# Talking-heads attention with a PReLU layer behind it: another order inside an attention step, and v's products in both places of one step

## The chip, the cores and the metric

The kernel runs on one core of a Trainium2 chip. The metric is the time of one execution in microseconds (us) on the device; less is better. In the profile PE is the engine that multiplies matrices (PEld its loads of weights), DVE the vector engine, ACT the scalar engine, POOL GpSimd and SP the engine that only issues transfers here.

## What is computed

Four batches of 12 heads, 448 positions, 64 numbers a head. Scores of all heads are mixed over the heads before the softmax, the probabilities once more after it, and the result goes through two layers with a PReLU between them. The shapes and the calls around it are left out:

```python
def _attn_ref(q, k, v, w_pre, w_post):
    scale = 1.0 / np.sqrt(q.shape[-1])
    scores = scale * np.matmul(q, k.transpose(0, 1, 3, 2))
    scores = np.einsum('bhij,hg->bgij', scores, w_pre)
    scores = scores - np.max(scores, axis=-1, keepdims=True)
    attn = np.exp(scores)
    attn = attn / (np.sum(attn, axis=-1, keepdims=True) + 1e-09)
    attn = np.einsum('bhij,hg->bgij', attn, w_post)
    return np.matmul(attn, v).astype(np.float32)

def _moe_ref(x, w_in, w_out, alpha):
    h = x @ w_in
    g = np.maximum(h, 0.0) + alpha * np.minimum(h, 0.0)
    return (g @ w_out).astype(np.float32)
```

x is (1792, 768), w_in (768, 2048), w_out (2048, 768); w_in, w_out and alpha come as 64-bit floats.

## The kernel before

Two stages follow each other: attention, which leaves x in DRAM (`x2`), and the two layers, which read it. The change touches the first alone.

The rows of queries are cut into 16 chunks (4 a batch, of 120, 120, 120 and 97 queries), and a chunk into groups of 10 queries times 12 heads, 120 partitions. A step takes two groups, the pair m; there are 90 pairs, and a chunk has six (the last of a batch four and a half). What happens to a pair, and where it stands in the code:

- `qk` (L138) multiplies q and k of a chunk, two heads at a time, six calls a chunk, into the tile `s`, two PSUM banks, of which there is one buffer (`ps_s`). `qk_out` (L149) is ACT's copy of it into `st`; I call it the evict of the scores.
- `relay` (L158), issued by POOL, moves `st` into a layout where the heads lie on partitions: tile `sr`.
- `mix` (L165) mixes the heads on PE: tile `m`, two buffers. `rmax` (L174) takes the row's maximum on DVE, `exp` (L179) the exponential on ACT, one half of the pair a call, `norm` (L186) the sums and the scaled mixing weights `r` on DVE.
- `post` (L197) mixes the probabilities on PE, into the tile `pa`, of which there is one buffer; `post_out` (L208) copies it on ACT, two copies, into `at` of its chunk.
- `pv` (L217) multiplies `at` with v, once all pairs of a chunk are through, in two halves of 48 matmuls in the profile's count, into the same one buffer of `ps_s` that the scores use; `pv_out` (L232) copies the sums on ACT after the second half, and a transfer takes them to `x2`.

The order is written out by hand (`manual_schedule`): each engine works off its instructions in the order in which the code emits them. `step(m)` (L378) emits one step: mixing of pair m + 1, `post` of pair m - 2, `norm` of m - 1, `rmax` of m + 1, the two `exp` of pair m, and what stands in the step's two places, (m, 0) and (m, 1). A place holds a `qk` or a half of `pv`, or nothing; the table `places` (L285 to L298) says what. `use(place, 0)` emits the products on PE and `use(place, 1)` the copy on ACT. The scores of a later chunk and v's products of an earlier one are so woven into the steps of the present one. Between them DVE rounds the 64-bit weights (`convert`, L250) at a fixed number of instructions a step, and SP issues the loads.

Of the kernel before, what the change touches and what calls it, by code (L numbers as in the profile page):

```python
# [36 lines left out]
LAG = 2  # L37
# [24 lines left out]
def talking_heads_prelu(ctx: ExitStack, tc: tile.TileContext, q, k, v, w_pre, w_post, mask, w_in, w_out, alpha, out):  # L62
# [102 lines left out]
    def mix(m):  # L165

        ps = ps_m.tile([128, 2, 512], F32, tag="m", name=f"m{m}")
        ga, gb = sr_t.pop(2 * m), sr_t.pop(2 * m + 1)
        for hf, g in ((0, ga), (64, gb)):
            for u, r in ((0, slice(0, 64)), (1, slice(64, SR0 + GP))):  # L170
                nc.tensor.matmul(ps[hf:hf + 64, u, :S], wk[r, :], g[r, :], start=True, stop=True)  # L171
        m_t[m] = ps

    def rmax(m):  # L174
        nm = sm.tile([128, 2], F32, tag="nm", name=f"nm{m}")
        nc.vector.tensor_reduce(out=nm, in_=m_t[m][:, :, :S], axis=AX.X, op=ALU.max, negate=True)  # L176
        nm_t[m] = nm

    def exp(m, u):  # L179
        if u == 0:  # L180
            e_t[m] = ep.tile([128, 2, S], F32, tag="e", name=f"e{m}")
            se_t[m] = sm.tile([128, 2], F32, tag="se", name=f"se{m}")
        nc.scalar.activation(out=e_t[m][:, u], in_=m_t[m][:, u, :S], func=AF.Exp, bias=nm_t[m][:, u:u + 1], scale=1.0,  # L183
                             accum_out=se_t[m][:, u:u + 1])

    def norm(m):  # L186
        se = se_t.pop(m)
        s1 = sm.tile([128, 2], F32, tag="s1", name=f"s1{m}")
        nc.vector.tensor_scalar_add(s1, se, 1e-9)
        nc.vector.reciprocal(out=s1, in_=s1)  # L190
        r = rp.tile([128, 2, HP], F32, tag="r", name=f"r{m}")
        wf = wq.rearrange("p (o g) i -> p o (g i)", o=1)
        nc.vector.tensor_tensor(r, wf.to_broadcast([128, 2, HP]),
                                s1.rearrange("p (u o) -> p u o", o=1).to_broadcast([128, 2, HP]), ALU.mult)
        r_t[m] = r

    def post(m):  # L197
        e, r = e_t.pop(m), r_t.pop(m)
        for u in range(2):
            for jb in range(NJ):  # L200
                s, c = divmod(jb, 2)
                for g in range(2):
                    h = slice(64 * g, 64 * g + 64)
                    dst = pa[64 * c:64 * c + 64, g, s * GP:(s + 1) * GP].rearrange("p (h i) -> p h i", h=H)
                    nc.tensor.matmul(dst[:, :, HI * u:HI * u + HI], e[h, u, 64 * jb:64 * jb + 64],  # L205
                                     r[h, u].rearrange("p (h i) -> p h i", h=H), start=True, stop=True)

    def post_out(m):  # L208
        for g in range(2):
            n = 2 * m + g  # L210
            ci, r = groups[n]
            if n == first[ci]:
                a_t[ci] = ap_.tile([128, NS, H, CW], F32, tag="a", name=f"at{ci}")
            dst = a_t[ci].rearrange("p s h i -> p (s h) i")[:, :, r * GI:(r + 1) * GI]
            nc.scalar.copy(dst, pa[:, g, :NS * GP].rearrange("p (s i) -> p s i", i=GI))  # L215
# [69 lines left out]
    places = {}  # L285
    for ci in range(NC):
        m = (first[ci + 1] - 1) // 2 + LAG + 1
        places[m, 1], places[m + 1, 0] = ("pv", ci, 0), ("pv", ci, 1)
    for ci in range(1, NC):
        m1 = laid_out(first[ci]) - 1  # L290
        m0 = laid_out(first[ci - 1]) + 1 if ci > 1 else -1
# [17 lines left out]
    with tc.manual_schedule():  # L309
# [52 lines left out]
        def relays(upto, dmas):  # L362
            nonlocal relayed
            while relayed < min(upto, NG):
                relay(relayed, dmas[relayed % len(dmas)])
                relayed += 1
# [3 lines left out]
        live = lambda m: 0 <= m < NB  # L370

        def use(place, out):
            if place in places:
                f, *args = places[place]
                {"qk": (qk, qk_out), "pv": (pv, pv_out)}[f][out](*args)


        def step(m):  # L378


            nonlocal done
            for f, *args in jobs.get(m, []):
                f(*args)
            if live(m + 1):
                mix(m + 1)
            now, later[:] = list(later), []
            for f in now:
                f()
            if live(m - LAG):
                post(m - LAG)  # L390
            if live(m - 1):
                norm(m - 1)
            if live(m + 1):
                rmax(m + 1)
            if live(m):
                exp(m, 0)
            use((m - 1, 1), 1)
            if m >= 0:
                relays(2 * (m + 2 + RAHEAD) if m > 2 else first[1], (nc.gpsimd,))
            if live(m):  # L400
                exp(m, 1)
            use((m, 0), 0)
            if live(m - LAG):
                post_out(m - LAG)
            use((m, 0), 1)
            use((m, 1), 0)
            want = (m + 1) * conv_steps // (NB - 4)
            while done < want and done < conv_steps:
                next(conv, None)
                done += 1  # L410

        last = max(m for m, _ in places)
        for m in range(-1, max(NB + LAG, last + 1) + 1):
            step(m)
# [144 lines left out]
```

## Time and profile before

| what | value |
|---|---|
| median of 3 runs | 953.32 us (939.89 to 953.99) |
| the profiled execution | 943.48 us, of which the span from first to last instruction is 941.7 us |
| PE busy in the span | 821.3 us (87%), 10,388 matmuls and 10,388 loads of weights |
| DVE, ACT, POOL busy | 486.7, 441.3, 355.6 us |
| granted clock of PE, mean | 0.976 of full speed |
| attention, from 38 to 456 us | PE 327.0, DVE 284.9, ACT 285.7 us busy in 418 us |
| the two layers, from 456 us | PE 470.3 us busy in 486 us |

A share of busy time is a mean over stages. The chain of waits and the timeline of a stretch tell what a change there is worth.

### The profile page before, as it was taken

The page shows a single profiled execution, that of the slowest core. Times are in us where ns is not written, and L with a number is a line of the kernel's source. Part 1 is how long each engine was busy: PE and PEld are TensorE (multiplying, and loading weights), DVE is VectorE, ACT ScalarE, POOL GpSimd, SP SyncE. Part 2 cuts the span into 40 slices and gives each one's busy share as a digit, 9 for nine tenths or more (in the row PEclk, how much of TensorE's full clock was granted, in tenths as well). Part 3 has the DMA queues.
Part 4 walks back from the last instruction along what each step waited for, and adds up shares of the span by engine and source line. Part 5 has one row for each costly group of instructions (what it writes and reads, how often), then busy time and mean ns, then how long its engine had stood idle before and what let it go on. Part 6 is the DMA issues. An engine that isn't in the chain of part 4 may idle for free.

```text
span 941.7 us, 23967 instructions
## 1 busy us (share of the span) xinstructions
PE 821.3 (87%) x10388; PEld 662.4 (70%) x10388; DVE 486.7 (52%) x856; ACT 441.3 (47%) x870; POOL 355.6 (38%) x315
## 2 busy tenths in 40 slices
PE   5766887778878888788399999999999999999998
PEld 3344555544645554456399999999999999999997
DVE  4756686677775686776242255322563226632222
ACT  1756776577675766776223322332223322332232
POOL 2321223122231232220244555455554555555442
PEclk9999999999998999999799999999999999999999
DMA  6997799967998688762592000200002000010001
GB/s 168 242 254 209 217 266 224 265 209 205 277 245 207 222 237 238 228 217 72 164 412 103 0 21 1 99 1 1 20 1 98 1 1 20 1 59 1 1 1 60
DMA packets 55158, 123.90 MB, mean 132 GB/s; under 512 B 26028, under 2 KB 32988, under 8 KB 55052
## 3 DMA queue, kind: packets, MB, share of 16 engines
q1 hardware_dynamic: 39846, 81.71, 29.0%
q0 software_dynamic: 14208, 37.56, 14.7%
q10 hardware_dynamic: 998, 3.09, 1.1%
q8 instruction: 82, 1.34, 0.6%
q14 instruction: 24, 0.20, 0.1%
HBM read 59.96 MB, written 23.62 MB: 89 GB/s over the span
## 4 chain that ended last, share of the span: by engine, by line
PE 66%; issue 15%; ACT 7%; POOL 4%; DMA 3%; DVE 3%; ACTq 0%; POOLq 0%; SPq 0%; DVEq 0%
PE h L463 25%; PE acc L488 25%; PE x L229 5%; PE pa L205 4%; POOL sr L163 4%; PE s L146 4%; PE m L171 3%; ACT st L154 3%; ACT at L215 2%; DMA sr<-st 2%; ACT e L183 1%; DVE nm L176 1%; DMA xr<-x 1%; DMA wb<-in_w_post_dram 1%; DVE ct L58 0%
## 5 line engine op out<-in xcount | busy, mean ns | idle before, releaser
L463 PE MATMUL h<-xs,wi 128*128 128x448 f32 x1152 | 247.0, 368 | 12.9 <-DVE xs L453 11.5
L488 PE MATMUL acc<-g,wo 128*128 128x448 f32 x1152 | 243.7, 365 | 0.0
L463 PEld LDWEIGHTS h<-xs,wi 128*128 128x128 f32 x1152 | 218.6, 190 | 31.0 <-issue 11.7
L488 PEld LDWEIGHTS acc<-g,wo 128*128 128x128 f32 x1152 | 216.4, 188 | 17.1
L163 POOL DMA_DIRECT2D sr<-st x174 | 108.8, 626 | 312.9 <-PE m L171 215.1
L441 POOL TENSOR_TENSOR wi<-wr,wi 128x768 fp32r<-128x768 f32 x64 | 118.8, 1856 | 253.2 <-ACT wi L440 253.2
L472 DVE TENSOR_SCALAR t<-h,alpha_sb 128x448 f32<-128x448 f32 x64 | 43.8, 684 | 236.8 <-PE h L463 236.8
L474 ACT CAST g<-t 128x448 fp32r<-128x448 f32 x64 | 36.3, 567 | 270.9 <-DVE t L473 270.9
L176 DVE TENSOR_REDUCE nm<-m 128x2 f32<-128x896 f32 x90 | 98.0, 1089 | 114.9 <-PE m L171 114.9
L205 PEld LDWEIGHTS pa<-r,e 64*64 64x64 f32 x5040 | 100.4, 135 | 77.6 <-issue 56.8
L146 PE MATMUL s<-k,q 64*64 64x448 f32 (+2 forms) x768 | 98.9, 561 | 57.2 <-ACT st L154 49.6
L205 PE MATMUL pa<-r,e 64*64 64x60 f32 x5040 | 104.6, 221 | 30.3 <-issue 25.8
L441 POOL TENSOR_TENSOR wo<-wr,wo 128x768 fp32r<-128x768 f32 x64 | 125.3, 1958 | 5.7 <-ACT wo L440 5.7
L215 ACT COPY at<-pa 128x480 f32<-128x480 f32 x180 | 93.2, 573 | 72.1 <-PE pa L205 67.9
L183 ACT ACTIVATE e<-m,nm 128x448 f32<-128x448 f32 x180 | 115.4, 648 | 4.7 <-DVE nm L176 2.9
L154 ACT COPY st<-s 120x896 f32<-120x896 f32 (+1 forms) x93 | 85.0, 914 | 44.2 <-PE s L146 44.0
L171 PE MATMUL m<-sr,wk 64*64 64x448 f32 x720 | 89.0, 558 | 7.6 <-DMA sr<-st 5.4
L229 PE MATMUL x<-at,v 128*64 128x120 f32 (+1 forms) x1536 | 88.3, 275 | 7.1 <-ACT st L154 3.5
L146 PEld LDWEIGHTS s<-k,q 64*64 64x64 f32 (+2 forms) x768 | 22.5, 128 | 99.0 <-ACT st L154 84.4
L229 PEld LDWEIGHTS x<-at,v 128*64 128x64 f32 x1536 | 81.3, 146 | 11.7 <-ACT st L154 5.8
L440 ACT CAST wo<-wr 128x768 fp32r<-128x768 f32 x64 | 53.5, 836 | 58.1 <-PE acc L488 58.1
L475 DVE TENSOR_TENSOR g<-t,g 128x448 fp32r<-128x448 f32 x64 | 40.8, 638 | 44.0 <-ACT g L474 44.0
(40 smaller groups left out, 482.8 us busy)
## 6 DMA issues: line engine op xcount, KB each, us to landing
sr<-st POOLq DMA_DIRECT2D x174, 210.0 KB, 6.6
cr<-in_w_in_dram SPq DMA_DIRECT2D x16, 768.0 KB, 7.6
cr<-in_w_out_dram SPq DMA_DIRECT2D x16, 768.0 KB, 6.6
wsc<-ct SPq DMA_DIRECT2D x32, 384.0 KB, 7.4
wr<-wsc SPq DMA_DIRECT2D x14, 768.0 KB, 10.5
xr<-x SPq DMA_DIRECT2D x24, 224.0 KB, 4.9
out_dram<-o SPq DMA_DIRECT2D x24, 224.0 KB, 2.0
k<-in_k_dram SPq DMA_DIRECT2D x21, 224.0 KB, 11.5
```

Of the source, the lines that this page charges most:

```text
L146: nc.tensor.matmul(ps[lo:hi, hf, :S], q_t[ci][r, p, lo:hi], k_t[b][r, p, :], start=True, stop=True)
L154: copy(dst[:cn, p], u_t.pop(("qk", ci, p))[:cn, :, :S])
L163: dma.dma_start(out=sr_t[n][SR0:SR0 + GP], in_=s_t[ci][r0:r0 + (GI - 1) * st + 1:st])
L171: nc.tensor.matmul(ps[hf:hf + 64, u, :S], wk[r, :], g[r, :], start=True, stop=True)
L176: nc.vector.tensor_reduce(out=nm, in_=m_t[m][:, :, :S], axis=AX.X, op=ALU.max, negate=True)
L183: nc.scalar.activation(out=e_t[m][:, u], in_=m_t[m][:, u, :S], func=AF.Exp, bias=nm_t[m][:, u:u + 1], scale=1.0, accum_out=se_t[m][:, u:u ...
L205: nc.tensor.matmul(dst[:, :, HI * u:HI * u + HI], e[h, u, 64 * jb:64 * jb + 64], r[h, u].rearrange("p (h i) -> p h i", h=H), start=True, s ...
L215: nc.scalar.copy(dst, pa[:, g, :NS * GP].rearrange("p (s i) -> p s i", i=GI))
L229: nc.tensor.matmul(ps[64 * t:64 * t + 64, half, cl * CW:cl * CW + cn], v_t[b][:, s, h * D:(h + 1) * D], a_t[ci][:, s, h, :cn], start=(s == ...
L441: nc.gpsimd.tensor_tensor(t[:, 1], w, t[:, 0], ALU.subtract)
L463: nc.tensor.matmul(ps[:, :S], w[:, tw, cc * 128:(cc + 1) * 128], x[:, tx, cc, :], start=(i == 0), stop=(i == 3 * NCC - 1))
L488: nc.tensor.matmul(accs[c][:, :S], w[:, tw, c * 128:(c + 1) * 128], g[:, tg], start=(f == 0 and i == 0), stop=(f == NFC - 1 and i == 2))
```

## The change

In `step` the calls are put into another order. Before, `post` follows the mixing, and ACT takes: first `exp`, evict of the last step's second place, second `exp`, `post_out`, evict of the first place. Now the evict of the last step's second place and the products of the first place come first, then both `exp`, the evict of the first place, `post`, the products of the second place, `post_out`. In the table, the two halves of v's products, so far in the second place of step m and the first of step m + 1, now stand in both places of step m. The places of the scores follow from what is left.

```diff
     for ci in range(NC):
         m = (first[ci + 1] - 1) // 2 + LAG + 1
-        places[m, 1], places[m + 1, 0] = ("pv", ci, 0), ("pv", ci, 1)
+        places[m, 0], places[m, 1] = ("pv", ci, 0), ("pv", ci, 1)
...
             for f in now:
                 f()
-            if live(m - LAG):
-                post(m - LAG)
+            use((m - 1, 1), 1)
+            use((m, 0), 0)
             if live(m - 1):
                 norm(m - 1)
             if live(m + 1):
                 rmax(m + 1)
             if live(m):
                 exp(m, 0)
-            use((m - 1, 1), 1)
+                exp(m, 1)
             if m >= 0:
                 relays(2 * (m + 2 + RAHEAD) if m > 2 else first[1], (nc.gpsimd,))
-            if live(m):
-                exp(m, 1)
-            use((m, 0), 0)
+            use((m, 0), 1)
+            if live(m - LAG):
+                post(m - LAG)
+            use((m, 1), 0)
             if live(m - LAG):
                 post_out(m - LAG)
-            use((m, 0), 1)
-            use((m, 1), 0)
```

ACT in a step with two score groups, from the evict of the first of them on, before (`st` the evict, `e` an exponential, `at` the copies of `post`):

```order
L154 COPY st_488<-s_2_551 120x2x448
L183 ACTIVATE e_611,se_612<-m_504,nm_542 128x448
L154 COPY st_488<-s_3_559 120x2x448
L183 ACTIVATE e_611,se_612<-m_504,nm_542 128x448
L215 COPY at_372<-pa 128x48x10 x2
```

The same place on ACT in the changed kernel:

```order
L154 COPY st_458<-s_2_510 120x2x448
L215 COPY at_372<-pa 128x48x10 x2
L154 COPY st_458<-s_3_557 120x2x448
L183 ACTIVATE e_589,se_590<-m_504,nm_520 128x448 x2
L154 COPY st_458<-s_4_577 120x2x448
```

The copies of `post` moved from behind the second exponential to between the two evicts, and the two exponentials follow each other.

PE around v's products of the first chunk, before (`m` the mixing, `pa` is `post`, `x` v's products, `s` scores):

```order
L171 MATMUL m_687<-sr_112,wk 64x448 x2
L171 MATMUL m_687<-sr_113,wk 64x448 x2
L205 MATMUL pa<-r_672,e_611 64x12x5 x28
L229 MATMUL x_736<-at_372,v_118 64x120 x24
L171 MATMUL m_770<-sr_114,wk 64x448 x2
L171 MATMUL m_770<-sr_115,wk 64x448 x2
L205 MATMUL pa<-r_723,e_676 64x12x5 x28
L229 MATMUL x_736<-at_372,v_118 64x120 x24
L171 MATMUL m_849<-sr_116,wk 64x448 x2
L171 MATMUL m_849<-sr_117,wk 64x448 x2
L205 MATMUL pa<-r_807,e_727 64x12x5 x28
L146 MATMUL s_0_896<-k_129,q_498 64x448 x2
```

The same place on PE in the changed kernel:

```order
L171 MATMUL m_687<-sr_112,wk 64x448 x2
L171 MATMUL m_687<-sr_113,wk 64x448 x2
L229 MATMUL x_692<-at_372,v_118 64x120 x24
L205 MATMUL pa<-r_645,e_589 64x12x5 x28
L229 MATMUL x_692<-at_372,v_118 64x120 x24
L171 MATMUL m_794<-sr_114,wk 64x448 x2
L171 MATMUL m_794<-sr_115,wk 64x448 x2
L146 MATMUL s_0_803<-k_129,q_498 64x448 x2
L146 MATMUL s_0_803<-k_129,q_498 33x448 x2
L205 MATMUL pa<-r_720,e_649 64x12x5 x28
```

Both halves of v's products stand in one step with one `post` between them, the step after it is already one with two score groups, and that one begins with its first scores, ahead of its `post`.

## Rows read from the trace of the kernel before

**Rows 1.** The page, 40 equal slices of the span: PE and the DMA engines, tenths.

```profile
PE   5766887778878888788399999999999999999998
...
DMA  6997799967998688762592000200002000010001
```

**Rows 2.** Chain of waits in a double step: start us, us, what.

```profile
410.16 0.97 PE s L146 x6
...
411.88 0.87 PE pa L205 x49
...
412.85 0.81 ACT at L215 x2
...
413.77 0.93 ACT st L154
...
414.74 0.97 PE s L146 x6
```

**Rows 3.** Timeline of PE, one round: start, us, instruction, idle before.

```profile
401.62 0.98 PE L171 MATMUL m<-sr,wk 64*64 64x448 f32 x8
...
415.53 0.93 PE L171 MATMUL m<-sr,wk 64*64 64x448 f32 x8
...
418.52 1.15 PE L205 MATMUL pa<-r,e 64*64 64x60 f32 x56 [0.16 <-ACT at L215]
419.60 2.68 PE L229 MATMUL x<-at,v 128*64 128x120 f32 x48
422.21 0.98 PE L171 MATMUL m<-sr,wk 64*64 64x448 f32 x8
...
426.65 0.98 PE L171 MATMUL m<-sr,wk 64*64 64x448 f32 x8
...
428.88 0.98 PE L171 MATMUL m<-sr,wk 64*64 64x448 f32 x8 [0.34 <-ACT e L183]
```

**Rows 4.** Waits of PE over the span: us in total, times, longest us.

```profile
PE pa L205 <- issue: 25.8, 15, 3.8
...
PE x L229 <- ACT st L154: 3.5, 3, 1.2
```

**Rows 5.** Chain of waits at 60 to 72 us.

```profile
59.72 3.30 issue
63.02 0.81 PE pa L205 x37
63.83 4.28 PE x L229 x48
68.10 0.91 PE m L171 x8
69.01 0.57 PE pa L205 x33
69.58 2.90 issue
```

**Rows 6.** The page, DMA queues: packets, MB, share of 16 engines.

```profile
q8 instruction: 82, 1.34, 0.6%
```

**Rows 7.** Timeline of ACT in the same round.

```profile
411.21 0.91 ACT L154 COPY st<-s 97x896 f32<-97x896 f32 x1 [0.47 <-PE s L146]
412.01 0.64 ACT L183 ACTIVATE e<-m,nm 128x448 f32<-128x448 f32 x1
...
418.36 0.64 ACT L183 ACTIVATE e<-m,nm 128x448 f32<-128x448 f32 x1
...
418.97 0.64 ACT L183 ACTIVATE e<-m,nm 128x448 f32<-128x448 f32 x1
...
419.72 1.03 ACT L215 COPY at<-pa 128x480 f32<-128x480 f32 x2
...
426.77 0.82 ACT L243 COPY xe<-x 128x360 f32<-128x360 f32 x2 [1.57 <-PE x L229]
...
428.09 0.65 ACT L183 ACTIVATE e<-m,nm 128x448 f32<-128x448 f32 x1
```

## The prediction

> **What bounds the kernel now.** I read the page first, for its slices [rows 1]: the second half of the span is one stretch of products of weights, PE at 9 tenths and over, and nothing of the change lies there. In the attention half PE stands at 5 to 8 tenths, so there the question is who waits for whom. I then read the waits of PE, the chain of waits inside one round of six steps, and the timeline of PE and of ACT through that round. I call a step with two score groups a double step, one with only mixing and `post` an empty step.
>
> In a double step the chain [rows 2] runs in a closed loop over two engines: the second score group (from 410.16), the mixing, `post`, then on ACT the copies of `post` (412.85), the evict of the first scores (413.77), and at 414.74 the next second score group. 414.74 - 410.16 = 4.58 us, and every piece of it is serial, because the scores have one PSUM buffer and because `post_out` stands ahead of the first scores' evict on ACT, and waits for a `post` that stands behind the mixing on PE.
>
> The whole round, from the mixing at 401.62 to the one at 426.65 [rows 3], takes 25.03 us: three double steps to 415.53 (13.91), then an empty step and two steps with a half of v's products each, to 426.65 (11.12). There are 14 such rounds (steps 4 to 87). In this round nothing but these waits holds PE.
>
> Elsewhere PE also stops where the trace names no releaser: 25.8 us in 15 waits ahead of `post` [rows 4]. Two of these stops follow each other in the chain [rows 5]: from the end of one at 63.02 to the start of the next at 69.58 stand 37 + 48 + 8 + 33 = 126 matmuls, each with a weight load, so about 252 instructions. The queue of instructions [rows 6] brought 82 packets of 1.34 MB in all, 16.3 KB each, and the page's 10,388 matmuls and as many loads make 253 instructions for each packet. So I read these stops as PE at the end of one packet of its program with the next not there yet. They come in the half in which the DMA engines are 6 to 9 tenths busy [rows 1]; in the second half, with the DMA engines nearly idle, PE has no such slice.
>
> By the Trainium skill (Runtime: NRT & Kernel Launch, Instruction fetch mechanics) the program is refilled in blocks of 16 KiB, 256 instructions, and crossing a block is mostly hidden. The trace agrees on the size of a block, and not on the cost, in the attention half: 3.30 and 2.90 us at two borders in a row. By the page's word the gain of the order would reach the end whole, and the forecast below would be 936.5 us; by the rows a part is lost again.
>
> **The change, part by part.** No instruction is added or taken away; two things are moved. I work with these durations, all from ACT's timeline [rows 7] and from [rows 2, 3]: second scores to the start of their evict 411.21 - 410.16 = 1.05; an evict to the next instruction of ACT 412.01 - 411.21 = 0.80; an evict to the score group that needs its bank 414.74 - 413.77 = 0.97; two exponentials to the next instruction 419.72 - 418.36 = 1.36, of which the first takes 0.61; second exponential to the mixing that needs its buffer 428.88 - 428.09 = 0.79; the copies of `post` 413.77 - 412.85 = 0.92; second scores to the next mixing 415.53 - 414.74 = 0.79.
>
> Double step, new order. Put zero where the second scores start. Their evict starts at 1.05, ACT then does both exponentials, and is free at 1.05 + 0.80 + 1.36 = 3.21. Meanwhile the first scores of the next step start at 1.05 + 0.97 = 2.02 and are ready at 3.07, before ACT is. The evict at 3.21 frees the bank, and the next second scores start at 3.21 + 0.97 = 4.18. `post` runs on PE beside this evict; its copies run on ACT beside the second scores, which is what the move wins: 4.18 for 4.58. The first double step after v's products starts with the copies of v's sums (0.82, at 0.12 after its mixing, 426.77 - 426.65) in place of an evict: 0.12 + 0.82 + 1.36 + 0.97 + 0.79 = 4.06 from mixing to mixing. Three double steps: 4.06 + 4.18 + 4.18 = 12.42 for 13.91, a gain of 1.49 a round.
>
> v's part. Both halves in one step leave two empty steps ahead of them instead of one. In the first, ACT has to evict the last scores before it may start the exponentials (before, the first of these stood ahead of the evict, in time that ACT waited anyway). From its mixing: evict at 1.05 - 0.79 = 0.26, second exponential at 0.26 + 0.80 + 0.61 = 1.67, and the next mixing, which needs the buffer it reads, at 2.46. ACT goes on with copies, 2.42 to 3.34, and the exponentials of the second empty step; the third mixing is at 3.34 + 0.61 + 0.79 = 4.74, so that step takes 2.28. The first half of v's products has to wait for the copies of that step, 3.34 + 1.36 + 0.92 = 5.62 and some 0.1 until PE sees it: 0.98 after the mixing. Then 2.61 (422.21 - 419.60), `post` about 1.05 (419.60 - 418.52 is 1.08), 2.61 again: the step takes 7.25. Sum 2.46 + 2.28 + 7.25 = 11.99 for 11.12, a loss of 0.87 a round. So I expect the two halves of this change to pull against each other.
>
> Round: 12.42 + 11.99 = 24.41 for 25.03, a gain of 0.62, times 14 = 8.7 us. Three of the rounds before have a score group and a half of v's products in one step, and pay an extra wait for an evict there, 3.5 us in 3 waits [rows 4]; with both halves in one step these go: 12.2. The two empty steps at the start, and the end of the stage, lose about 0.5 each as an empty step does above: 11.2 us of gain.
>
> Against this stand the stops for the program. In a round 528 matmuls go in 25.03 us, a packet's 126 in 5.97; after, in 5.83. Where a packet is late anyway, these 0.14 us come back as a longer stop, and a few packets that just came in time no longer do. With 15 stops in [rows 4], a few more ahead of other matmuls, and as much again for new ones I take 2.5 us. What they may do is bounded by the rows: from -26 (all of them gone) to +43 (one more of 3.1 us, the mean of the two in [rows 5], in each of 14 rounds). I stay near nothing, since the number of packets and the mean rate hardly change.
>
> Waits that I cost at nothing: `post` now stands behind the first scores, its copies can start 1.20 us after it does (419.72 - 418.52), and ACT comes to them at about the same moment, so this cover is thin; if it goes, 0.1 us a double step, 4 us in all. POOL's relays keep their place among the evicts.
>
> Sum: 943.48 - 11.2 + 2.5 = 934.8 against the profiled execution. That one stands 9.8 us under the median, 953.32; of the four times shown (939.89, 943.48, 953.32, 953.99) the mean is 947.7, 4.2 above it. I put the forecast in the middle of such a scatter: 934.8 + 4.2 = 939 us, 1.5% under the median. A measurement of this kernel can tell about 2% from no change, so this is "the same" by a little.
>
> **The rivals.**
>
> More than the chain says. If a more even flow lets the packets land in time (before, an empty step and one with v's products ask for a packet in about 4.8 us), half of the 26 us go, and with the slow matmuls after a stop (48 of v's products in 4.28 us in [rows 5], against 2.61) some 17 us. 939 - 17 = 922. For it: the stops are gathered in v's part. Against it: two empty steps in a row ask for 128 matmuls in 4.74 us, as dense as before. Chance 0.17.
>
> Nothing arrives. The stops, not the waits for evicts, set the pace over most of the stage, and every gain returns as a longer stop. Then the times stay where they were, 944 to 956, middle 950. For it: the scatter of the times shown is larger than the whole gain. Against it: the round in [rows 3] is held by nothing but evicts. Chance 0.18.
>
> Slower. The dense stretch of two empty steps and two halves of v's products, 288 matmuls in 12 us, outruns its packets each time: PE stops once more per round, within `post` between the two halves. It decides as soon as a packet takes over 4.7 us, the time of the two empty steps, from being asked for to being there. Price 14 x 3.1 = 43 us less the 11 gained: 948 + 32 = 980 us. Against it: before, the densest stretch ran as fast and stopped in a part of the rounds only. Chance 0.05.
>
> **How the numbers follow.** The forecast has 0.60, and 931 to 948 as its own range. Faster by over 2% means under 934.3: the first rival's 0.17 and a fifth of the forecast's, 0.12, together 0.29. Slower by over 2% is over 972.4: 0.05. The rest, 0.66, lies within 2%. For 8 times in 10 the range takes in most of the second rival and the upper part of the first: 924 to 954.
>
> **What would show it.** In the chain of a double step: second scores to second scores 4.2 us instead of 4.58, PE's wait for the evict still there, the copies of `post` gone from the loop. Two empty steps of 2.3 to 2.5 us, then a step of 7.2. In the waits: PE behind no named releaser 20 to 35 us. The forecast is wrong in its steps if a double step stays at 4.5 or more, or if the first half of v's products starts over 1.5 us after its mixing, and wrong in its sum if the unnamed stops change by more than 12 us.

## The result, and the profile after

| | before | changed |
|---|---|---|
| median | 947.83 us (936.86 to 958.02, 20 runs) | 932.32 us (925.97 to 945.24, 20 runs) |
| ratio, 95% interval | | 0.9867 (0.9839 to 0.9895) |
| profiled execution; its span | 943.48; 941.7 us | 936.22; 934.4 us |

The ratio is worth 12.6 us (10.0 to 15.3): a gain that 20 runs separate from nothing, and less than 2%. The forecast was 939 us in a range of 924 to 954, and "within 2%" with 0.66.

The page after, 40 equal slices in tenths, against [rows 1]:

```profile
PE   5779897798779989875699999999999999999998
```

PE stands higher in the attention half, mostly at 7 to 9 tenths where it had 6 to 8. The slice where the products of weights begin has 6 for 3, because they begin earlier in it.

The timeline of PE through one whole round that no stop disturbs (start, us, instruction, idle before), against [rows 3]:

```profile
189.97 0.93 PE L171 MATMUL m<-sr,wk 64*64 64x448 f32 x8
...
192.43 0.98 PE L171 MATMUL m<-sr,wk 64*64 64x448 f32 x8 [0.60 <-ACT e L183]
...
194.59 0.98 PE L171 MATMUL m<-sr,wk 64*64 64x448 f32 x8
195.50 2.68 PE L229 MATMUL x<-at,v 128*64 128x120 f32 x48
198.11 1.15 PE L205 MATMUL pa<-r,e 64*64 64x60 f32 x56
199.19 2.68 PE L229 MATMUL x<-at,v 128*64 128x120 f32 x48
201.80 0.98 PE L171 MATMUL m<-sr,wk 64*64 64x448 f32 x8
...
204.87 0.98 PE L146 MATMUL s<-k,q 64*64 64x448 f32 x8
205.67 0.93 PE L171 MATMUL m<-sr,wk 64*64 64x448 f32 x8
206.88 0.98 PE L146 MATMUL s<-k,q 64*64 64x448 f32 x8 [0.28 <-ACT st L154]
207.68 1.09 PE L205 MATMUL pa<-r,e 64*64 64x60 f32 x56
208.91 0.98 PE L146 MATMUL s<-k,q 64*64 64x448 f32 x8
...
213.76 0.93 PE L171 MATMUL m<-sr,wk 64*64 64x448 f32 x8
```

Read it from mixing (`m`) to mixing: empty steps of 2.46 and 2.16, v's step of 7.21, the first double step 3.87, and two more that end at 213.76. The round takes 23.79 us, 25.03 before: 1.24 saved. From second scores to second scores, 204.87 to 208.91, it is 4.04 where [rows 2] had 4.58, and `post` (207.68) runs while ACT evicts the first scores. That is the move that the diff describes.

ACT in the same double step, against [rows 7]:

```profile
205.92 0.91 ACT L154 COPY st<-s 120x896 f32<-120x896 f32 x1
206.72 0.64 ACT L183 ACTIVATE e<-m,nm 128x448 f32<-128x448 f32 x1
207.34 0.64 ACT L183 ACTIVATE e<-m,nm 128x448 f32<-128x448 f32 x1
207.95 0.91 ACT L154 COPY st<-s 120x896 f32<-120x896 f32 x1
208.82 1.04 ACT L215 COPY at<-pa 128x480 f32<-128x480 f32 x2
209.96 0.91 ACT L154 COPY st<-s 120x896 f32<-120x896 f32 x1
```

The timeline marks no idle time ahead of any of them: ACT is now the loop's busy engine. The two exponentials take 207.95 - 206.72 = 1.23.

The waits of PE after (us in total, times, longest), against [rows 4]:

```profile
PE x L229 <- issue: 19.8, 9, 4.5
PE s L146 <- ACT st L154: 11.9, 33, 1.1
PE m L171 <- ACT e L183: 10.4, 16, 1.2
...
PE pa L205 <- issue: 9.0, 7, 2.2
```

The same list of before has this line for the evict of the scores:

```profile
PE s L146 <- ACT st L154: 49.6, 44, 1.3
```

Some 38 us of waiting for the evict went, and 8 came back as waits of a mixing for the exponential, 10.4 where they were 2.0 (192.43 above is one). The stops without a named releaser moved from `post` into v's products, and their sum stayed: 28.8 us against 29.4.

### The profile page after: what moved, and what is told of

Its sections match the earlier page's. It is cut to its first block, busy times and chain, and to the rows that moved or that the text cites. A ratio compares the mean times of both kernels' runs of the same rounds, so it can differ in the third digit from the quotient of the medians.

```text
span 934.4 us, 23967 instructions
## 1 busy us (share of the span) xinstructions
PE 840.6 (90%) x10388; PEld 665.0 (71%) x10388; DVE 486.1 (52%) x856; ACT 438.1 (47%) x870; POOL 355.8 (38%) x315
## 4 chain that ended last, share of the span: by engine, by line
PE 69%; ACT 12%; issue 9%; DMA 5%; DVE 3%; POOL 1%; SPq 0%; ACTq 0%; POOLq 0%; DVEq 0%
PE acc L487 25%; PE h L462 25%; PE x L229 9%; ACT e L183 6%; PE s L146 4%; ACT st L154 4%; PE pa L205 3%; DMA sr<-st 3%; PE m L171 2%; ACT at L215 2%; DMA xr<-x 1%; POOL sr L163 1%; DMA wb<-in_w_post_dram 1%; DVE nm L176 1%; DVE ce L57 0%
## 5 line engine op out<-in xcount | busy, mean ns | idle before, releaser
L462 PE MATMUL h<-xs,wi 128*128 128x448 f32 x1152 | 251.1, 371 | 13.7 <-DVE xs L452 12.1
L487 PE MATMUL acc<-g,wo 128*128 128x448 f32 x1152 | 248.3, 368 | 0.0
L205 PEld LDWEIGHTS pa<-r,e 64*64 64x64 f32 x5040 | 102.5, 138 | 55.4 <-issue 33.8
L205 PE MATMUL pa<-r,e 64*64 64x60 f32 x5040 | 106.8, 225 | 14.4 <-issue 9.0
L146 PE MATMUL s<-k,q 64*64 64x448 f32 (+2 forms) x768 | 100.7, 577 | 19.3 <-ACT st L154 11.9
L171 PE MATMUL m<-sr,wk 64*64 64x448 f32 x720 | 92.6, 566 | 18.5 <-ACT e L183 10.4
L229 PEld LDWEIGHTS x<-at,v 128*64 128x64 f32 x1536 | 77.8, 140 | 36.6 <-issue 21.9
## 6 DMA issues: line engine op xcount, KB each, us to landing
wr<-wsc SPq DMA_DIRECT2D x14, 768.0 KB, 10.2
```

The costliest lines, as they stand in the source:

```text
L146: nc.tensor.matmul(ps[lo:hi, hf, :S], q_t[ci][r, p, lo:hi], k_t[b][r, p, :], start=True, stop=True)
L229: nc.tensor.matmul(ps[64 * t:64 * t + 64, half, cl * CW:cl * CW + cn], v_t[b][:, s, h * D:(h + 1) * D], a_t[ci][:, s, h, :cn], start=(s == ...
L462: nc.tensor.matmul(ps[:, :S], w[:, tw, cc * 128:(cc + 1) * 128], x[:, tx, cc, :], start=(i == 0), stop=(i == 3 * NCC - 1))
L487: nc.tensor.matmul(accs[c][:, :S], w[:, tw, c * 128:(c + 1) * 128], g[:, tg], start=(f == 0 and i == 0), stop=(f == NFC - 1 and i == 2))
```

## The experiments

The stage in the table below runs from the mixing of step 1 to that of step 88, in one profiled execution each. "Stops" are PE's idle times there without a named releaser, "the rest" is the stage less these. The last column is the part of the stage that the granted clock of PE was short of full speed: 1 less its mean over the stage, times the stage. It counts idle time at the low clock too, so it is an upper bound of what PE lost; the last section needs it. The first seven lines leave nothing out; the last four are the "light" kernels, without most of the weights' transfers.

| kernel | stage | stops | the rest | lost to the clock |
|---|---|---|---|---|
| before; again (e10) | 405.5; 402.1 | 29.4; 28.7 | 376.1; 373.4 | 10.2; 6.8 |
| changed; again (e9, e11) | 387.1; 383.8, 393.5 | 28.8; 32.8, 31.9 | 358.3; 351.0, 361.6 | 11.9; 8.6, 17.1 |
| e1, order alone | 376.1 | 27.3 | 348.8 | 13.7 |
| e2, places alone | 401.1 | 27.9 | 373.2 | 8.5 |
| e5, order, early exponential | 374.6 | 29.8 | 344.8 | 10.2 |
| e6, order, `post` first | 404.7 | 22.1 | 382.6 | 6.8 |
| e7, PE's order alone | 459.1 | 3.2 | 455.9 | 46.1 |
| e3, before, light | 369.5 | 1.3 | 368.2 | 3.4 |
| e4, changed, light | 358.6 | 10.9 | 347.7 | 3.4 |
| e8, order alone, light | 348.6 | 3.8 | 344.8 | 3.4 |
| e12, places alone, light | 374.6 | 5.3 | 369.3 | 5.1 |

**The two parts apart.** First the new order with the old places:

```diff
-        places[m, 0], places[m, 1] = ("pv", ci, 0), ("pv", ci, 1)
+        places[m, 1], places[m + 1, 0] = ("pv", ci, 0), ("pv", ci, 1)
```

> The new order inside a step, with v's halves left in (m, 1) and (m + 1, 0). By the prediction (the order wins 1.49 us a round, the places lose 0.87): 14 x 0.87 = 12 us faster than the changed kernel, about 920 us, ratio to before 0.971. Rival, that most of that loss belongs to the order itself (the evict that now stands ahead of the first exponential in the first empty step) and little to the places: within 4 us of the changed kernel, 928 to 936, ratio 0.98 to 0.988. Rival, that the places are what wins: no change, 945 to 950. In all three by the first two a double step takes 4.0 to 4.2 us.

Measured: 923.81 us, 0.9809 (0.9771 to 0.9847). The prediction's own figure, 0.971, lies outside the interval; the ratio is the first rival's, with 5.5 us to the changed kernel by the ratios where it had at most 4. Its timeline of PE, a whole round:

```profile
364.62 0.93 PE L171 MATMUL m<-sr,wk 64*64 64x448 f32 x8
367.07 0.98 PE L171 MATMUL m<-sr,wk 64*64 64x448 f32 x8 [0.60 <-ACT e L183]
...
371.68 0.98 PE L171 MATMUL m<-sr,wk 64*64 64x448 f32 x8
...
376.08 0.59 PE L171 MATMUL m<-sr,wk 64*64 64x448 f32 x2
...
380.31 0.93 PE L171 MATMUL m<-sr,wk 64*64 64x448 f32 x8
...
388.41 0.93 PE L171 MATMUL m<-sr,wk 64*64 64x448 f32 x8
```

388.41 - 364.62 = 23.79, to the hundredth the round of the changed kernel. So the places win or lose nothing in such a round, and the wait of 0.60 at the second mixing is there with the old places too. Inside the round they shift time: e1's empty step and two steps with v's products take 2.45 + 4.61 + 4.40 = 11.46, the changed kernel's 11.83; e1's first double step takes 4.23, the changed kernel's 3.87.

The other part alone, the diff's one line of places in the kernel before:

> v's halves in both places of one step, the old order inside a step. By the prediction: a double step stays at 4.58 us, the empty steps and v's step lose up to 0.87 us a round, so 948 to 960, ratio 1.00 to 1.013. Rival, that the order carries the loss: 945 to 950, ratio 0.997 to 1.003. Rival, that the places win by gathering PE's stops in fewer steps: 936 or less, ratio under 0.988.

Measured: 946.22 us, 1.0026 (0.9999 to 1.0053): no difference. The double step keeps the old loop, 380.44 - 375.85 = 4.59, with the old wait (timeline of PE):

```profile
375.85 0.98 PE L146 MATMUL s<-k,q 64*64 64x448 f32 x8 [1.16 <-ACT st L154]
...
380.44 0.98 PE L146 MATMUL s<-k,q 64*64 64x448 f32 x8 [1.18 <-ACT st L154]
```

By the times the whole gain is the order's.

**What the stops are.** Kernel before, with the transfers of the weights left out:

```diff
-            if i < len(todo):
-                f, x = todo[i]
-                raw_c[i] = cvp.tile([128, DM], I64, tag="cr", name=f"cr{f}_{x}")
-                nc.sync.dma_start(out=raw_c[i], in_=(w_in, w_out)[x][f])
+            if i == 0:
+                raw_c[0] = cvp.tile([128, DM], I64, tag="cr", name="cr0")
+                nc.sync.dma_start(out=raw_c[0], in_=w_in[0])
...
-            later.append(lambda f=f, x=x, t=t: store_c(f, x, t))
```

> The kernel before without the loads and stores of the 64-bit weights in the attention stage (all roundings work on the first slice, the layers read a piece of v in place of the weights): 37 of the stage's some 92 MB are left out. If PE's unnamed stops are its program coming late behind other transfers, they fall from 28 us to under 6, and the time falls by more than they do, since the matmuls after a stop run at the lower granted clock: 905 to 922. If they are PE's own (its queue, its rate), they stay at 20 us or more and the time stays at 940 to 950.

Measured: 923.09 us, 0.9778 (0.974 to 0.9817). The waits of PE in the stage hold these lines, where [rows 4] had 25.8 us ahead of `post`:

```profile
PE pa L205 <- issue: 0.7, 2, 0.4
PE m L171 <- issue: 0.6, 1, 0.6
```

The program is as long; with the other transfers gone, 28 of 29 us of stops go. Where the stops stand says the same. Count PE's instructions in a trace from its start (matmuls, loads of weights and the few that only wait for semaphores): each of the 180 stops in the stages of the fourteen traces stands 193 or 194 behind a multiple of 256, so always at the same place of a stretch as long as a packet of the program (253 in the prediction's count, which leaves the waiting ones out). So a stop is a part of the program that comes late because of the other transfers; whether these hold it up in the DMA engines or in the memory isn't separated. The time missed the expectation by a little: it fell by 21 us, less than the stops, to 923 where 922 was the most. In the profiled execution, the fastest of the four, the stage fell by 36 us (33 against e10), and behind it PE ran at the slower of two paces that are described below, 9 us more. The Trainium skill (Runtime: NRT & Kernel Launch, Instruction fetch mechanics) says that crossing a block is mostly hidden: true here in this light kernel, not in the kernel itself.

Then the changed kernel, and in two further runs each part alone, with the same transfers left out:

> The changed kernel with the same transfers left out. If the stops gave back a part of what the order won, this one is 17 to 22 us faster than the light kernel before (14 rounds of 1.25 us less, and the three rounds with an extra wait), more than the 12.6 us between the full kernels. If nothing was given back, the two light kernels differ by 11 to 14 us as the full ones do.

> e1 without the transfers of the weights in the attention stage, as in e3 and e4. If e1 beats the changed kernel by its chain (a round of 23.6 for 23.8 us, the rounds with a score group beside v's, the tail), it is 4 to 7 us under e4, ratio 0.957 to 0.960. If it beats it because it stops less for its program with v's products spread over two steps, its stops are under 4 us here against 10 in e4, and with the chain it is 8 to 14 us under e4, ratio 0.949 to 0.956.

> e2 (places alone, old order) without the transfers of the weights, the fourth of the light kernels. If the places bring the stops that e4 has and e8 and e3 have not, PE's unnamed stops in the attention stage are 6 to 11 us here and the time is 3 to 12 us over e3. If it is order and places together (a shorter round that asks for the program faster), they stay under 4 us here and the time is that of e3 within 4 us.

Measured: e4 909.06 us, 0.9636 (0.9602 to 0.9671); e8 893.8 us, 0.9435 (0.9351 to 0.9518); e12 916.67 us, 0.9694 (0.9592 to 0.9796). From e3 to e4 the medians fall by 14.0 us (by the ratios 13.4), against 15.5 (12.6) with all transfers. By the times alone nothing is given back to the stops. The traces are less simple: the rest of the stage fell by 20.5, and stops rose from 1.3 to 10.9. With the new order the places cost time here: e4's interval lies clear above e8's, and e4 has 10.9 us of stops for e8's 3.8. The medians are 15 us apart, more than either theory had; in the two profiled executions the stages are 10.0 apart, of which the stops are 7.1. With the old order (e12 beside e3) the intervals overlap, and e12's 5.3 us of stops lie between what the two theories expected: undecided. That e12's median lies 6 us under e3's, which neither had, need not come from the places: in the profiles its stage is 5.1 us longer than e3's, and its second half ran at the faster of the two paces below.

**Is it PE's order or ACT's?** In the order alone, `post` back ahead of the first place, ACT's order kept new:

```diff
             use((m - 1, 1), 1)
+            if live(m - LAG):
+                post(m - LAG)
             use((m, 0), 0)
...
-            if live(m - LAG):
-                post(m - LAG)
```

> e1 with ACT in the new order, but post back ahead of the first scores on PE. If the gain needs the first scores ahead of post, the loop becomes second scores, mixing, post, first scores, evict: a double step of 4.4 to 4.5 us, and the first one after v's products over 5, ratio 1.00 to 1.03. If moving the copies on ACT alone wins (they stand behind the evict here too), the double step stays at 4.0 to 4.1 us and the ratio at 0.98.

Measured: 946.79 us, 1.0038 (1.0002 to 1.0073). The gain is gone; double step 168.60 - 164.16 = 4.44, and the first one behind v's products 404.82 - 399.16 = 5.66, for 4.74 before (timeline of PE):

```profile
164.16 0.98 PE L146 MATMUL s<-k,q 64*64 64x448 f32 x8 [1.03 <-ACT st L154]
...
168.60 0.98 PE L146 MATMUL s<-k,q 64*64 64x448 f32 x8 [1.03 <-ACT st L154]
...
399.16 0.98 PE L171 MATMUL m<-sr,wk 64*64 64x448 f32 x8
401.09 1.09 PE L205 MATMUL pa<-r,e 64*64 64x60 f32 x54 [0.94 <-ACT at L215]
```

The 0.14 that a double step still wins is lost again in that step, where `post` waits for the copies of the `post` before it, and in the empty step, which keeps the 2.45 of e1 (1.84 before).

The other half, again as an edit of the order alone: PE's order new, on ACT the whole old order, with the copies of `post` ahead of the first scores' evict:

```diff
+            if live(m):
+                exp(m, 0)
             use((m - 1, 1), 1)
...
-            if live(m):
-                exp(m, 0)
-                exp(m, 1)
...
-            use((m, 0), 1)
+            if live(m):
+                exp(m, 1)
             if live(m - LAG):
                 post(m - LAG)
-            use((m, 1), 0)
-            if live(m - LAG):
                 post_out(m - LAG)
+            use((m, 0), 1)
+            use((m, 1), 0)
```

> The opposite half: PE in the new order (first scores ahead of post), ACT in the old one (first exponential, evict, second exponential, copies of post, evict). If both halves are needed, the copies wait for the later post and the evict stands behind them: second scores 1.05, evict 0.97, first scores 0.8, post 1.15, copies 0.92, evict 0.97, a double step of about 5.8 us, ratio 1.04 to 1.06. If the order on PE alone wins, 4.1 to 4.6 us.

Measured: 1009.87 us, 1.0688 (1.0596 to 1.0779), 2 runs. Double step 182.33 - 176.49 = 5.84 (timeline of PE), as expected; the time at the upper end or above it:

```profile
176.49 0.98 PE L146 MATMUL s<-k,q 64*64 64x448 f32 x8 [1.93 <-ACT st L154]
...
182.33 0.98 PE L146 MATMUL s<-k,q 64*64 64x448 f32 x8 [1.93 <-ACT st L154]
```

First scores now wait for the second's evict, `post` for the first scores, its copies for `post`, and the first evict for these: one loop without any overlap. PE's half alone costs 7%, ACT's half alone wins nothing, both together win.

**The order's own loss.** In e1, the first exponential ahead of the evict in a step whose first place is empty:

```diff
+            early = live(m) and (m, 0) not in places
+            if early:
+                exp(m, 0)
             use((m - 1, 1), 1)
```

> e1 (order alone) with one more move: in a step whose first place is empty the first exponential goes ahead of the evict of the last step. If the first empty step's 2.46 us come from that evict, it falls to about 2.2 us, 0.27 a round and 4 us in all: ratio to before 0.977, some 920. If that step is held by something else (the maximum on DVE, the mixing's own), nothing changes: 0.981.

Measured: 920.99 us, 0.9762 (0.9708 to 0.9817), the lowest time of the kernels that leave nothing out. The empty step falls from 2.45 (e1) to 215.08 - 212.85 = 2.23, the wait from 0.60 to 0.37 (timeline of PE):

```profile
212.85 0.93 PE L171 MATMUL m<-sr,wk 64*64 64x448 f32 x8
215.08 0.98 PE L171 MATMUL m<-sr,wk 64*64 64x448 f32 x8 [0.37 <-ACT e L183]
```

So this part of the loss, 0.22 of some 0.6 (1.84 before), is ACT's evict ahead of the first exponential; the rest is open. The time isn't separated from e1's. It is from the changed kernel's: the two intervals don't meet.

**What of the span doesn't belong to the change.** The span fell by 7.3 us while the stage fell by 18.4. Both kernels once more, and the changed one a third time:

> The changed kernel once more, for the pace of the second half, which the change doesn't touch: 18 matmuls of weights took 3.65 us in the profile before and 3.72 us in the one after, 9 us over the half. If the kernel's order sets this pace, 3.72 here, in both looks at the changed kernel, and 3.65 in the look at the one before. If it is drawn anew in every execution, the four looks (with the two above) don't sort by kernel. The attention stage, from the mixing of step 1 to that of step 88: 380 to 392 us by either.

> The kernel before once more, for the same question: 3.65 us if the kernel sets the pace, either of the two if each execution draws it. The attention stage from step 1 to step 88: 400 to 410 us.

> The changed kernel a third time, behind the other one on the same chip: 3.72 us again if the kernel sets the pace; if it was set by what ran before on the chip or by chance, it need not be.

Measured: 929.15, 939.56 and 936.21 us. One piece of the chain of waits in the second half, 18 matmuls, in the changed kernel's first profile:

```profile
610.48 3.72 PE acc L487 x18
```

and in e9, the same kernel:

```profile
617.07 3.65 PE acc L487 x18
```

All three take 3.65; of the eleven other profiles six show 3.65 (before, e1, e2, e5, e6 and, in the light kernels, e12) and the rest 3.72, so the kernel doesn't set it. There are 128 such pieces (2 x 1152 matmuls by 18), 0.07 x 128 = 9 us: most of the 11 us that the first profile lost outside the stage.

The rest of them does belong to the change. It stands between the stage and the layers, from the mixing of step 88 (437.77 before, 418.81 after) to PE's first product of weights (timeline of PE, before, then after):

```profile
466.06 0.71 PE L463 MATMUL h<-xs,wi 128*128 128x448 f32 x1 [11.52 <-DVE xs L453]
```

```profile
449.78 0.71 PE L462 MATMUL h<-xs,wi 128*128 128x448 f32 x1 [12.12 <-DVE xs L452]
```

That is 28.3 us before (28.4 in e10) and 31.0 in the changed kernel, 33.0 and 34.0 in e9 and e11. So 3 to 6 us of what the stage wins are lost behind it, which fits a gain of 15.7 us in the stages (mean of all profiles of both kernels) and of 12.6 in the times.

## Why the prediction was right, and where it was wrong

**The loop: right, its size too small.** The double step was foretold at 4.18 and is 4.04, the first after v's products 4.06 and is 3.87. The mis-sized term is the pair of exponentials, "two exponentials to the next instruction 1.36". The row behind it ran to ACT's next instruction, and that was the copies of `post`, for which ACT had first to wait. The pair itself takes 1.23, and 4.18 - 0.13 = 4.05 is what came. It counts in each of 42 double steps, and in the second of two empty ones: the round won 1.24 and not 0.62. "11.2 us of gain" became 18.4 in the profiled stage; by all profiles of both, 403.8 to 388.1, it is 15.7. That the move needs both engines was argued from the loop in [rows 2], and e6 and e7 show it.

**v's part: right sum, wrong cause.** The steps of 2.46, 2.28 and 7.25 came as 2.46, 2.16 and 7.21, and `x` starts 0.91 after its mixing (0.98 foretold). But "a loss of 0.87 a round" was put on the new places, and from it came "the two halves of this change pull against each other". e1 has the same 23.79 with the old places. In the round the loss is the order's: in the first empty step, 2.45 for 1.84, the evict of the last scores, now ahead of the first exponential, delays it, and e5 gets back 0.22 of it by that one edit. What the new places lose beside that in v's steps (11.83 for e1's 11.46) they win back in the first double step (3.87 for 4.23). The step that failed is that I worked out the new order and the new places together in these three steps, and laid the difference on the part that stood nearest. Another term was too small: "the end of the stage" was to lose about 0.5, and the way from step 88 to the first product of weights is longer by 2.7 in the first profile, by 4.6 to 5.7 in e9 and e11.

**The places.** With the new order they still cost: about 0.6% or 5.5 us between e1 and the changed kernel (intervals that overlap a little, 0.9839 to 0.9847), and clearly between e8 and e4. The 3.5 us of "these go" were laid on the places, and the order alone brings them: the three rounds that had scores beside a half of v's products (steps 13 to 18, 36 to 41, 58 to 63) take, where no stop falls in them, 25.91 before, 25.20 with the places alone, 23.96 with the order alone (e1, e8) and 23.8 to 24.2 with both. In three other rounds (steps 18 to 23, 41 to 46, 63 to 68) it is 23.28 with the order alone (e8) and 24.0 to 24.3 with both, some 2.4 us in the three against the places, and in the last six steps of the stage (82 to 87) 20.2 (e1, e8) and 21.4 (e4), 1.2 more. The rest of the cost of the places is open. That two halves in one step ask for the program more densely would fit 10.9 against 3.8 us of stops in the light kernels, from one execution each; with all transfers it isn't seen (28.8 to 32.8 against 27.3 and 29.8).

**The stops: sum right, meaning right.** 20 to 35 us were foretold and 28.8 to 32.8 came. That "these come back as a longer stop" (2.5 us) is within what single executions scatter by. In e7, which takes the longest, stops fall to 3.2 us; that a slower loop leaves the program time to arrive would fit, but was not tried by itself. The rival by which the stops set the pace and no gain arrives is refuted by e1 and by the ratio itself; the one by which half of the stops go has no support in the rows, and its 17 us weren't worked out (13 of stops leave 4 for slow matmuls, where 4.28 - 2.61 = 1.67 behind each of seven stops would be 12); the one with a new stop in each dense stretch decided nowhere near 43 us, but nine stops of up to 4.5 us now do stand in v's products.

**The sum.** 934.8 against the profiled execution, which took 936.22, looks like a hit by 1.4 us. It is luck, two errors that cancel: the stage fell by 18.4 us where 11.2 - 2.5 = 8.7 had been foretold, and outside it 11.1 were lost, 9 of them because the second half happened to run at the slower pace. Against many runs it is simpler: the net gain of 8.7 us was too small, 12.6 by the ratio and 15.5 by the medians, and the forecast of 939 was 6.7 too high.

## What to carry to other kernels

Where one buffer is passed between two engines, draw the closed loop over both and move the instructions on both at once: here one engine's half of the move was worth nothing, and the other's cost 7%. When two edits share a step, work out each one alone, and run each alone, before laying a loss on one of them. Compare stages, not spans, when a gain of 1% is judged from single executions, and look for what differs in a stage that the change doesn't touch.

## What the runs showed of the hardware that was not expected

**A program that comes late.** In the attention stage some 15,200 instructions of PE took 27 to 33 us of stops in the kernels before, changed, e1, e2 and e5, with the DMA engines busy for 0.82 to 0.88 of the stage, and 1.3 to 10.9 us in the light kernels, with 0.55 to 0.60. Every stop stands at the same place of a stretch of 256 instructions. A stop can have a tail, too. The chain of the changed kernel at one stop, against [rows 5]:

```profile
138.59 1.85 PE x L229 x43
140.44 4.52 issue
144.96 0.39 PE x L229 x5
145.35 1.64 PE m L171 x8
```

The mixing behind it takes 1.64 where 0.98 is usual. Stretches of the same place (from:to, us, PE busy and matmuls, granted clock, DMA share, GB/s) show why:

```profile
140.40:144.90 4.50, 0.04 (x1) 1.00 1.02 258
144.90:146.40 1.50, 1.44 (x13) 0.69 1.05 281
146.40:147.00 0.60, 0.60 (x8) 0.50 0.87 234
147.00:149.00 2.00, 2.00 (x42) 0.53 1.03 238
149.00:152.00 3.00, 2.64 (x60) 1.00 0.87 249
```

After 4.5 us without work PE goes on at full clock at first, then for some 3 us at half of it, the 1.2 GHz level, and then at full speed again. [rows 5] have the same: v's products take 4.28 behind the stop of 3.30, with 0.57 granted. Not every stop does this: behind the next one there, of 2.90, the granted clock stays at 1.00. By the table all low stretches together are 6.8 to 17.1 us of a stage in the kernels with all transfers but e7; how much of that is due to stops is not separated. In e7 the waits of the loop come before it (same view):

```profile
204.00:208.00 4.00, 1.82 (x64) 1.00 1.04 287
208.40:209.40 1.00, 1.00 (x12) 1.00 0.51 195
209.40:211.00 1.60, 1.60 (x12) 0.51 0.01 4
```

PE was busy 1.82 of 4.00 us there, with a wait of 1.93 at its end, and ran at half the clock soon after. Over its stage that makes 46.1 us, which may be why its ratio came out at the upper end of the expectation or above; that was not tried by itself.

**Two paces at one clock.** The matmuls of the second half run at 3.65 or 3.72 us for 18, 203 or 207 ns each, with a granted clock of 1.00 in both. A profiled execution keeps one of them, and no edit here chose it. What does is open.
